# Another token layout for k and v from unit 6 on, and a load behind a store

## The chip, the core and the metric

The kernel runs on one core of a Trainium2 chip. The metric is the device time of one execution in microseconds; the time before is the median of 3 runs. A profile of one further execution goes with it. The engines are named as in the profile: PE is TensorE's matmul, PEld its weight load, DVE is VectorE, ACT is ScalarE, POOL is GpSimd, SP is SyncE, which here only issues DMAs.

## What is computed

The first half is a retention layer: for each of 4 batches and 8 heads, over 768 tokens of 64 features, a 64 x 64 state is decayed and updated, and a query reads it.

```python
gamma = 1.0 - 2.0 ** (-5.0 - np.arange(H))
for t in range(S):
    state = gamma[None, :, None, None] * state + np.einsum('bhd,bhe->bhde', k[:, :, t], v[:, :, t])
    y[:, :, t] = scale * np.einsum('bhd,bhde->bhe', q[:, :, t], state)
```

The second half takes y as 3072 tokens of 512 features through a feed-forward layer: `h = x @ w_in` (512 to 2048), `g = max(h, 0) + alpha * min(h, 0)`, and `g @ w_out` (2048 to 512). Inputs and output are float32.

## The kernel before

**Units and blocks.** A unit (`u`, 0 to 11) is 256 tokens of one batch, three units to a batch. Inside a unit there are two chunks of 128 tokens (`c`). A block (`n`, 0 to 5) is two units, 512 tokens, and is what the feed-forward layer takes at once. While PE works on the feed-forward of block n, the attention of the units of block n + 1 (`u0 = 2 * (n + 1)` and `u0 + 1`) is put in between: the feed-forward parts are generators, `tick(gen, m)` emits m matmuls of them. The order of the program is the order on each engine and each DMA queue; everything is written out by hand.

**A unit's preparation.** `load` brings q, k and v of a unit from DRAM by SP, one DMA of 512 KB each (the first units in halves). Partition p of the staged tile holds tokens 2p and 2p + 1 of the unit, all 8 heads; a run of 512 contiguous bytes per head. So partitions 0 to 63 hold the first chunk and 64 to 127 the second (`rows(c)`), and r = 0 or 1 tells a partition's two tokens apart. `rescale` multiplies q and k with powers of gamma from the table `tab` and casts them to float16 (`kdq`); `cast_v` casts v (`vx`). From unit 4 on this is POOL's work. `turn_dma` transposes `kdq` into `kq` with a DMA on SP (the earlier units with PE in `turn_pe`), so that features lie on partitions. `kdq`, `kq` and `vx` have 4 buffers each, the staged tiles 3.

**A unit's attention.** All of it uses 64 x 64 quarters of PE's array, four matmuls at a time (two chunks c, two heads a of a pair p):

- `sum_mm` (L215): the state's update of each chunk, k against v, 64 columns.
- `score_mm` (L268): for each half r of a chunk's keys, the 64 keys against all 128 queries of the chunk; 16 matmuls a call, two calls (`hh`) a unit.
- `masks` (L280): DVE multiplies the scores of 512 columns, both halves r, with the causal mask `mi`; four a unit.
- `out_mm`: the state's part (L298, whole array), then the masked scores against v (L313), 32 matmuls of 128 columns, added up in PSUM.
- `state_sum` (L237 to L241) adds and decays the running state on DVE and POOL; `state_copy` puts it into float16 tiles `tg`.

The queries' order inside a chunk is all even tokens, then all odd ones; `take_y` (ACT) puts the output back into place in `xT`.

**The feed-forward.** `ffn1` (L378) makes 16 tiles of h in 64 matmuls, ACT and DVE apply the activation (L389, L391). For block 0 `ffn2` does the second product; from block 1 on `ffn2_seven` (L464) does it as seven products of 16 matmuls in place of eight, with sums of g made by `g_sums` (L362). Their results are stored by SP (L489, `store`): output tile (0,0) in the second product, then (1,1), (1,0) and (0,1). The output tiles `os` have three buffers.

**SP's queue.** For block 1 it holds, in this order: the transposes of units 4 and 5, the loads of units 6 and 7, the four stores of block 1. From block 2 to 3: transpose of `u0`, load of `u0 + 2`, transpose of `u0 + 1`, load of `u0 + 3`, four stores. A DMA that waits holds up what is queued behind it.

Of the kernel before, what the change touches and what calls it, by code (L numbers as in the profile page):

```python
# [10 lines left out]
F16 = mybir.dt.float16  # L11
# [10 lines left out]
def kernel(  # L22
# [10 lines left out]
    nc = tc.nc  # L33
# [3 lines left out]
    NP = H // 2  # L37


    U = 256  # L40
    UPB = S // U
    NU = B * UPB
# [6 lines left out]


    OQ, OD, OI = 2 * H, 4 * H, 4 * H + NP
    NTAB = OI + NFT
    tab_np = np.zeros((128, NTAB), dtype=np.float64)
    for h in range(H):
        for r in range(2):
            j = 2 * (p_ar % 64) + r
            tab_np[:, 2 * h + r] = g64[h] ** (127.0 - j)
            tab_np[:, OQ + 2 * h + r] = scale * g64[h] ** (j + 1.0 - 128.0)
    for p in range(NP):
        tab_np[0:64, OD + p] = g64[2 * p] ** 128  # L60
# [10 lines left out]
    mi = sbp.tile([128, 512], F16, tag="mi", name="mi")  # L71
    mask = mi[:, 0:256].rearrange("p (r i) -> p r i", r=2)
    ident = mi[:, 256:384]
    dec = tab[:, OD : OD + NP].unsqueeze(2).to_broadcast([128, NP, 64])
    alpha_sb = sbp.tile([NFT, 128], FP, tag="alpha", name="alpha")
    spin = sbp.tile([128, 512], F16, tag="spin", name="spin")
# [33 lines left out]
    def hold(ins):  # L110
        if held:
            tc.add_manual_dep(
                ins.ins,
                held.pop().ins.name,
                mybir.DependencyInfo(
                    mybir.DependencyClass.Sync, mybir.DependencyReason.DATA
                ),
                reason="loads behind weights",
            )

    def load(u, parts="kqv"):
        b, c = divmod(u, UPB)
        t = staged.setdefault(u, {})
        for nm in parts:
            src = {"k": k, "q": q, "v": v}[nm[0]]
            if nm[0] not in t:
                t[nm[0]] = sbp.tile(
                    [128, H, 2 * D], FP, tag=f"{nm[0]}s", bufs=3, name=f"{nm[0]}s{u}"
                )
            h = slice(0, H) if len(nm) == 1 else slice(4 * int(nm[1]), 4 * int(nm[1]) + 4)  # L130
            hold(
                nc.sync.dma_start(  # L132
                    out=t[nm[0]][:, h, :],
                    in_=src[b, h, U * c : U * c + U, :].rearrange(
                        "h (p r) d -> p h (r d)", r=2
                    ),
                )
            )

    def unit(u):  # L140
        if u not in prepped:
            prepped[u] = (
                sbp.tile([128, 2, 2, H, D], F16, tag="kdq", bufs=4, name=f"kdq{u}"),
                sbp.tile([128, 4 * NP, 128], F16, tag="kq", bufs=4, name=f"kq{u}"),
                sbp.tile([128, H, 2, D], F16, tag="vx", bufs=4, name=f"vx{u}"),
            )
        return prepped[u]

    def rescale(eng, u, t, h0, h1):
        kdq = unit(u)[0]  # L150
        at = OQ * t
        return eng.tensor_tensor(  # L152
            out=kdq[:, t, :, h0:h1, :].rearrange("p r h d -> p h r d"),
            in0=staged[u]["kq"[t]][:, h0:h1, :].rearrange("p h (r d) -> p h r d", r=2),
            in1=tab[:, at + 2 * h0 : at + 2 * h1]
            .rearrange("p (h r) -> p h r", r=2)
            .unsqueeze(3)
            .to_broadcast([128, h1 - h0, 2, D]),
            op=MULT,
        )  # L160
# [13 lines left out]
    def turn_pe(u, hh, bank):  # L174
# [17 lines left out]
            bias=0.0,  # L192
            scale=1.0,
        )

    def rows(x):
        return slice(64 * x, 64 * x + 64)
# [29 lines left out]
    def state(u, c, eng, copy="gg"):  # L227

        state_copy(state_sum(u, c, eng), copy)
# [28 lines left out]
    def score_mm(u, hh, banks):  # L258
        _, kq, _ = prepped[u]
        kv = kq.rearrange("p (t r a) i -> p t r a i", t=2, r=2)  # L260
        scs = [ps(banks[0], "sca"), ps(banks[1], "scb")]
        for r in range(2):
            for pp in range(2):
                p = 2 * hh + pp
                for c in range(2):
                    for a in range(2):
                        at = 256 * r + 128 * pp
                        nc.tensor.matmul(  # L268
                            out=scs[a][rows(c), at : at + 128],
                            lhsT=kv[rows(a), 0, r, p, rows(c)],  # L270
                            rhs=qmove(kq, a, c, p),
                            start=True,
                            stop=True,
                        )
        live[u, hh] = scs

    def masks(u, hh, parts=(0, 1)):
        for a in parts:
            m2 = sbp.tile([128, 2, 2, 128], F16, tag=f"m2{a}{hh}", bufs=2, name=f"m2{a}{hh}")
            i = nc.vector.tensor_tensor(  # L280
                out=m2,
                in0=live[u, hh][a].rearrange("p (r a i) -> p r a i", r=2, a=2),
                in1=mask.unsqueeze(2).to_broadcast([128, 2, 2, 128]),
                op=MULT,
            )
            live[u, hh][a] = m2
        return i

    def out_mm(u, banks, evict=True):
        _, kq, vx = prepped[u]  # L290
        ys = [ps(banks[0], "y0"), ps(banks[1], "y1")]
        inter = [(u, c) in tgs for c in range(2)]
        assert inter == [u % UPB > 0, True]

        for c in range(2):
            for p in range(NP):
                if inter[c]:
                    nc.tensor.matmul(  # L298
                        out=ys[c][:, 128 * p : 128 * p + 128],
                        lhsT=tgs[u, c][:, p, :],  # L300
                        rhs=kq.rearrange("p (t r a) i -> p t r a i", t=2, r=2)[
                            :, 1, :, p, rows(c)
                        ],
                        start=(p == 0),
                        stop=False,
                        skip_group_check=True,
                    )
        for p in range(NP):
            m2s = live[u, p // 2]
            for r in range(2):  # L310
                for c in range(2):
                    for a in range(2):
                        nc.tensor.matmul(  # L313
                            out=ys[c][rows(a), 128 * p : 128 * p + 128],
                            lhsT=vx[rows(c), 2 * p + a, r, :],
                            rhs=m2s[a][rows(c), r, p % 2, :],
                            start=(r == 0 and p == 0 and not inter[c]),
                            stop=(r == 1),
                            skip_group_check=True,
                        )  # L320
        live[u] = ys
        if evict:
            take_y(u, (0, 1))
# [237 lines left out]
    load(1, ("k0", "q0", "k1", "q1", "v0", "v1"))  # L561
    V.memset(spin, 1.0)
    V.memset(mi, 1.0)
    V.memset(warm, 0.0)
    A.activation(out=warm, in_=warm, func=RELU, bias=0.0, scale=-1.0)

# [4 lines left out]
    for x in range(2):  # L571
        m = mi[rows(x), 0:256].rearrange("p (j i t) -> p j i t", j=2, i=2)
        G.affine_select(
            out=m, in_=m, pattern=[[-1, 2], [1, 2], [2, 64]], compare_op=NOT_LESS,
            fill=0.0, base=0, channel_multiplier=-2,
        )
    for t in tgbuf:
        V.memset(t, 0.0)

# [116 lines left out]
    turn_dma(4)  # L696
    turn_dma(5)
    load(6)
    load(7)
    tick(half)  # L700


    for n in range(1, NBLK):
# [17 lines left out]
        if more:  # L721
            tick(gen, 8)
            sum_mm(u0, (2, 3))
            sum_mm(u0 + 1, (2, 3), half=1)
            score_mm(u0, 0, (4, 5))
            score_mm(u0, 1, (6, 7))
            state(u0, 0, G)
            masks(u0, 0)
            s01 = state_sum(u0, 1, G)
            masks(u0, 1, (0,))  # L730
            s10 = state_sum(u0 + 1, 0, G)
            masks(u0, 1, (1,))
# [50 lines left out]
```

## Time and profile before

| what | value |
|---|---|
| median of 3 runs | 204.73 us (204.58 to 204.78) |
| the profiled execution | 206.04 us, span 204.3 us |
| PE busy | 195.2 us (96%), 2314 matmuls |
| DVE busy | 157.0 us (77%) |
| ACT, POOL busy | 101.9 us (50%), 83.3 us (41%) |
| granted TensorE clock | 1.000 |
| chain that ended last | PE 73%, DMA 16%, DVE 3%, POOL 2% |
| `score_mm` matmuls (L268) | 384 of 64 columns by 128, 4 at a time |
| masks (L280) | 48, about 683 ns each |
| unit loads of 512 KB | ks 4.6, qs 5.5, vs 6.4 us from issue to landing (median) |
| transposes by DMA | 8, 3.8 us to landing (median) |

The span runs from the first to the last instruction; the time of the execution has what lies around it as well. A digit in the slices is the busy share of a fortieth of the span in tenths. A line of the chain or of a timeline gives the start, the length, the engine, the line and, with "x", how many instructions were merged. A matmul's length is its whole passage; what a stream of them costs is read from the distance of their starts.

### The profile page before, as it was taken

What the parts mean: (1) busy time and instruction counts of PE and PEld (TensorE: products, weight loads), DVE (VectorE), ACT (ScalarE), POOL (GpSimd) and SP (SyncE); (2) the same over time, 40 slices, a digit from 0 to 9 for tenths busy, and PEclk for the clock granted to TensorE, in tenths of its full rate; (3) what the DMA queues carried; (4) which work ended last, traced back from release to release, by engine and by line L of the source; (5) the groups of instructions that cost most, each with busy time, mean ns of one, the idle gap of its engine ahead of it and who ended that gap; (6) DMA issues with size and microseconds to landing.
All of it is one profiled execution on the core that took longest, in us unless ns stands there. A gap on an engine that the chain in (4) does not pass through costs nothing.

```text
span 204.3 us, 5491 instructions
## 1 busy us (share of the span) xinstructions
PE 195.2 (96%) x2314; PEld 128.2 (63%) x2314; DVE 157.0 (77%) x246; ACT 101.9 (50%) x169; POOL 83.3 (41%) x96
## 2 busy tenths in 40 slices
PE   7789997999999999999999999999999999999993
PEld 2457543566574788744788644788544888545882
DVE  7794985646899999189998289996489995589841
ACT  2465665236376333477353466333476254466311
POOL 2289117480269553970065960165930250000000
PEclk9999999999999999999999999999999999999999
DMA  5998999599997799399911499910570011200004
GB/s 158 337 234 134 185 253 235 157 249 173 299 346 223 153 340 304 110 258 304 284 46 41 149 250 281 300 55 22 176 166 0 3 52 57 103 0 0 21 33 154
DMA packets 64696, 33.94 MB, mean 166 GB/s; under 512 B 18064, under 2 KB 64160, under 8 KB 64672
## 3 DMA queue, kind: packets, MB, share of 16 engines
q1 hardware_dynamic: 60272, 29.37, 50.0%
q0 software_dynamic: 4224, 4.19, 13.4%
q8 instruction: 18, 0.29, 0.6%
q10 hardware_dynamic: 176, 0.03, 0.1%
q14 instruction: 6, 0.05, 0.1%
HBM read 27.30 MB, written 6.29 MB: 164 GB/s over the span
## 4 chain that ended last, share of the span: by engine, by line
PE 73%; DMA 16%; DVE 3%; POOL 2%; SPq 2%; issue 2%; ACT 0%; POOLq 0%; DVEq 0%
PE hps L378 32%; PE ox L464 16%; PE oy L464 11%; DMA qs<-in_q_dram 6%; PE ops L416 5%; DMA wout<-in_moe_w_out_dram 4%; DMA win<-in_moe_w_in_dram 4%; DMA ks<-in_k_dram 3%; PE y L313 2%; SPq L132 2%; PE sca L268 2%; PE y L298 1%; POOL tf L241 1%; PE st L215 1%; PE oz L464 1%
## 5 line engine op out<-in xcount | busy, mean ns | idle before, releaser
L378 PE MATMUL hps<-xT,win 128*128 128x512 f16 (+1 forms) x432 | 84.5, 355 | 0.1
L391 DVE SCALAR_TENSOR_TENSOR gt<-hm,oma,hps 128x512 f16<-128x512 f32 (+1 forms) x108 | 70.8, 685 | 13.6 <-ACT hm L389 8.1
L389 ACT ACTIVATE hm<-hps 128x512 f32<-128x512 f32 x96 | 57.3, 597 | 33.6 <-PE hps L378 31.4
L378 PEld LDWEIGHTS <-win 128*128 128x128 f16 x432 | 42.0, 98 | 40.3 <-DMA win<-in_moe_w_in_dram 0.8
L464 PEld LDWEIGHTS <-gs 128*128 128x128 f16 x320 | 31.0, 98 | 3.9
L241 POOL TENSOR_TENSOR tf<-ss,tab 128x256 f32<-128x256 f32 x16 | 12.2, 765 | 35.7 <-DVE ss L240 34.7
L464 PEld LDWEIGHTS <-gt 128*128 128x128 f16 x240 | 22.8, 98 | 4.8
L152 POOL TENSOR_TENSOR kdq<-ks,tab 128x1024 f16<-128x1024 f32 (+1 forms) x10 | 17.3, 1729 | 18.8 <-issue 9.8
L480 ACT ACTIVATE cu<-ox 128x512 f32<-128x512 f32 (+1 forms) x18 | 9.5, 526 | 29.9 <-PE ox L464 29.7
L256 POOL CAST tg<-tf 64x256 f16<-64x256 f32 x29 | 14.2, 488 | 20.0 <-DVE tf L237 18.6
L485 DVE TENSOR_TENSOR os<-oy,cu 128x512 f32<-128x512 f32 x14 | 9.6, 689 | 16.2 <-PE oy L464 13.7
L152 POOL TENSOR_TENSOR kdq<-qs,tab 128x1024 f16<-128x1024 f32 (+1 forms) x13 | 20.7, 1594 | 1.9 <-DMA qs<-in_q_dram 1.9
L280 DVE TENSOR_TENSOR m<-sca,mi 128x512 f16<-128x512 f32 x24 | 16.4, 684 | 4.2 <-PE scb L268 4.2
L464 PE MATMUL ox<-wsum,gs 128*128 128x256 f16 x160 | 19.1, 273 | 0.0
L331 ACT ACTIVATE xT<-y 128x512 f16<-128x512 f32 x24 | 16.2, 741 | 5.6 <-PE y L313 5.5
L280 DVE TENSOR_TENSOR m<-scb,mi 128x512 f16<-128x512 f32 x24 | 16.3, 681 | 0.0
L416 PE MATMUL ops<-wout,gt 128*128 128x512 f16 x64 | 15.2, 380 | 0.2 <-DMA wout<-in_moe_w_out_dram 0.2
L168 POOL CAST vx<-vs 128x1024 f16<-128x1024 f32 (+1 forms) x13 | 12.5, 973 | 5.6 <-DMA vs<-in_v_dram 5.6
L362 DVE TENSOR_TENSOR gs<-gt 128x1024 f16<-128x1024 f16 (+1 forms) x14 | 12.9, 922 | 0.3
L254 ACT ACTIVATE tg<-tf 64x256 f16<-64x256 f32 x11 | 4.6, 414 | 15.6 <-POOL tf L241 10.4
L188 ACT ACTIVATE kq<-trb 128x1024 f16<-128x1024 f16 x8 | 8.2, 1024 | 6.7 <-PE trb L182 6.5
L464 PE MATMUL ox<-wout,gt 128*128 128x256 f16 x80 | 10.4, 274 | 0.0
(50 smaller groups left out, 175.1 us busy)
## 6 DMA issues: line engine op xcount, KB each, us to landing
out_dram<-os SPq DMA_DIRECT2D x21, 256.0 KB, 2.3
vs<-in_v_dram SPq DMA_DIRECT2D x10, 512.0 KB, 6.4
ks<-in_k_dram SPq DMA_DIRECT2D x8, 512.0 KB, 4.6
qs<-in_q_dram SPq DMA_DIRECT2D x8, 512.0 KB, 5.5
ks<-in_k_dram SPq DMA_DIRECT2D x8, 256.0 KB, 4.7
qs<-in_q_dram SPq DMA_DIRECT2D x8, 256.0 KB, 4.8
win<-in_moe_w_in_dram POOLq DMA_DIRECT2D x4, 512.0 KB, 8.0
wout<-in_moe_w_out_dram POOLq DMA_DIRECT2D x4, 512.0 KB, 8.5
```

Of the source, the lines that this page charges most:

```text
L152: return eng.tensor_tensor(out=kdq[:, t, :, h0:h1, :].rearrange("p r h d -> p h r d"), in0=staged[u]["kq"[t]][:, h0:h1, :].rearrange("p h ...
L168: eng.tensor_copy(out=o, in_=i)
L241: eng.tensor_tensor(out=t, in0=ss, in1=dec, op=MULT)
L256: nc.gpsimd.tensor_copy(out=o, in_=i)
L280: i = nc.vector.tensor_tensor(out=m2, in0=live[u, hh][a].rearrange("p (r a i) -> p r a i", r=2, a=2), in1=mask.unsqueeze(2).to_broadcast([ ...
L331: nc.scalar.activation(out=xT[n][:, ul, :, 128 * c : 128 * c + 128].rearrange("k a (p r) -> k a r p", r=2), in_=ys[c].rearrange("k (a r p) ...
L362: return nc.vector.tensor_tensor(out=o, in0=a, in1=b, op=op)
L378: nc.tensor.matmul(out=hps[:, f, :].rearrange("p (u t) -> p u t", t=U), lhsT=w_in_all[:, hp, 128 * (f0 + f) : 128 * (f0 + f) + 128], rhs=x ...
L389: nc.scalar.activation(out=hm, in_=hps, func=RELU, bias=0.0, scale=-1.0)
L391: nc.vector.scalar_tensor_tensor(out=gt[:, f0 + f, U * lo : U * hi], in0=hm[:, f, :], scalar=oma_sb[:, f0 + f : f0 + f + 1], in1=hps[:, f, :],
L416: nc.tensor.matmul(out=opss[tq], lhsT=gt[:, ft, 128 * tq : 128 * tq + 128], rhs=w_out_all[:, ft, :], start=(ft == 0), stop=(ft == NFT - 1),)
L464: nc.tensor.matmul(out=o[1][m], lhsT=lhs(f, m), rhs=rhs(f), start=(first and f == 0 and (m == 0 or o[0] is None)), stop=(f == HF - 1), ski ...
```

## The change

From `SPLIT = 6` on, that is for units 6 to 11:

- k and v are loaded in another layout. Partition p of the lower half holds tokens p and p + 64 of the first chunk, the upper half those of the second chunk. Each of the two tensors comes in 4 DMAs, one for each chunk (x) and half of its tokens (y), on 64 partitions, with 256 contiguous bytes a head and 128 KB a DMA. q keeps its layout and its one DMA.
- r = 1 now means the second 64 tokens of a chunk. No query of the first 64 sees them, so `score_mm` and `out_mm` take only the 64 later queries for r = 1. In the query order that is the columns 32 to 63 of the even and of the odd tokens: two pieces of 32 columns in what `score_mm` reads and in what `out_mm` adds to. The scores of r = 1 lie at column 256 with 64 columns a pair.
- `masks` multiplies 384 columns in place of 512, with a mask of its own, `mj`, that is made at the start by one memset on DVE and four selects on POOL.
- `rescale` of k takes other powers of gamma, a further 16 columns of the table.

For all units: `kdq`, `kq` and `vx` have 3 buffers in place of 4. And the load of unit 7 is no longer issued right behind that of unit 6, but in the loop's first pass (n = 1), where the emitted products have put the first store of block 1 on SP's queue ahead of it.

```diff
+    SPLIT = 6
...
-    NTAB = OI + NFT
+    O2 = OI + NFT
+    NTAB = O2 + 2 * H
...
+            tab_np[:, O2 + 2 * h + r] = g64[h] ** (127.0 - (p_ar % 64 + 64 * r))
...
+            if u >= SPLIT and nm != "q":
+                for x in range(2):
+                    for y in range(2):
+                        at = U * c + 128 * x + 64 * y
+                        nc.sync.dma_start(
+                            out=t[nm][rows(x), :, D * y : D * y + D],
+                            in_=src[b, :, at : at + 64, :].rearrange("h p d -> p h d"),
+                        )
+                continue
...
-                sbp.tile([128, 2, 2, H, D], F16, tag="kdq", bufs=4, name=f"kdq{u}"),
-                sbp.tile([128, 4 * NP, 128], F16, tag="kq", bufs=4, name=f"kq{u}"),
-                sbp.tile([128, H, 2, D], F16, tag="vx", bufs=4, name=f"vx{u}"),
+                sbp.tile([128, 2, 2, H, D], F16, tag="kdq", bufs=3, name=f"kdq{u}"),
+                sbp.tile([128, 4 * NP, 128], F16, tag="kq", bufs=3, name=f"kq{u}"),
+                sbp.tile([128, H, 2, D], F16, tag="vx", bufs=3, name=f"vx{u}"),
...
-        at = OQ * t
+        at = OQ if t else (O2 if u >= SPLIT else 0)
...
-                        at = 256 * r + 128 * pp
+                        at, n, q = 256 * r + 128 * pp, 128, qmove(kq, a, c, p)
+                        if u >= SPLIT and r == 1:
+                            at, n, q = 256 + 64 * pp, 64, q[:, :, 32:64]
                         nc.tensor.matmul(
-                            out=scs[a][rows(c), at : at + 128],
+                            out=scs[a][rows(c), at : at + n],
                             lhsT=kv[rows(a), 0, r, p, rows(c)],
-                            rhs=qmove(kq, a, c, p),
+                            rhs=q,
...
+            m2 = sbp.tile([128, 512], F16, tag=f"m2{a}{hh}", bufs=2, name=f"m2{a}{hh}")
+            if u >= SPLIT:
+                i = nc.vector.tensor_tensor(
+                    out=m2[:, 0:384], in0=live[u, hh][a][:, 0:384], in1=mj, op=MULT
+                )
...
+                        o = ys[c][rows(a), 128 * p : 128 * p + 128]
+                        at, n = 256 * r + 128 * (p % 2), 128
+                        if u >= SPLIT and r == 1:
+                            at, n = 256 + 64 * (p % 2), 64
+                            o = o.rearrange("p (r i) -> p r i", r=2)[:, :, 32:64]
                         nc.tensor.matmul(
-                            out=ys[c][rows(a), 128 * p : 128 * p + 128],
+                            out=o,
                             lhsT=vx[rows(c), 2 * p + a, r, :],
-                            rhs=m2s[a][rows(c), r, p % 2, :],
+                            rhs=m2s[a][rows(c), at : at + n],
...
     V.memset(mi, 1.0)
+    V.memset(mj, 1.0)
     V.memset(warm, 0.0)
...
+        for lo, n in ((0, 64), (256, 32)):
+            m = mj[rows(x), lo : lo + 4 * n].rearrange("p (a i t) -> p a i t", a=2, i=2)
+            G.affine_select(
+                out=m, in_=m, pattern=[[0, 2], [1, 2], [2, n]], compare_op=NOT_LESS,
+                fill=0.0, base=0, channel_multiplier=-1,
+            )
...
     load(6)
-    load(7)
     tick(half)
...
             tick(gen, 17)
+            if n == 1:
+                load(7)
             state(u0 + 1, 1, G)
```

More of the change, by code (lines that the diff above doesn't have):

```diff
@@ L73 @@
     ident = mi[:, 256:384]
+    mj = sbp.tile([128, 512], F16, tag="mj", name="mj")[:, 0:384]
     dec = tab[:, OD : OD + NP].unsqueeze(2).to_broadcast([128, NP, 64])
@@ L119, in hold, with rows @@
             )
+    def rows(x):
+        return slice(64 * x, 64 * x + 64)
     def load(u, parts="kqv"):
@@ L194, in turn_pe @@
         )
-    def rows(x):
-        return slice(64 * x, 64 * x + 64)
     def qmove(kq, a, c, p):
@@ L278, in masks @@
         for a in parts:
[L279 to L285, printed above, removed]
+            m2 = sbp.tile([128, 512], F16, tag=f"m2{a}{hh}", bufs=2, name=f"m2{a}{hh}")
[3 more added lines that the diff above has]
+                )
+            else:
+                i = nc.vector.tensor_tensor(
+                    out=m2.rearrange("p (r a i) -> p r a i", r=2, a=2),
+                    in0=live[u, hh][a].rearrange("p (r a i) -> p r a i", r=2, a=2),
+                    in1=mask.unsqueeze(2).to_broadcast([128, 2, 2, 128]),
+                    op=MULT,
+                )
             live[u, hh][a] = m2
@@ L576 @@
         )
+        for lo, n in ((0, 64), (256, 32)):
[3 more added lines that the diff above has]
+                fill=0.0, base=0, channel_multiplier=-1,
+            )
     for t in tgbuf:
```

## The prediction

> **What bounds the kernel now.** I read the page's slices first, then the chain that ended last, then the timelines of TensorE, VectorE and SP around one block.
>
> ```profile
> span 204.3 us, 5491 instructions
> ...
> PE   7789997999999999999999999999999999999993
> ...
> DVE  7794985646899999189998289996489995589841
> ...
> PEclk9999999999999999999999999999999999999999
> DMA  5998999599997799399911499910570011200004
> ```
>
> From about 60 us on, PE stands at 9 in every slice but the last, at full granted clock, while DMA falls to 0 or 1 in many slices. The chain, for the block that starts at 115 us:
>
> ```profile
> 115.12 13.81 PE hps L378 x64
> 128.93 0.91 PE ox L464 x8
> 129.84 0.62 PE st L215 x42
> ...
> 135.83 0.57 PE y L313 x32
> ...
> 144.84 1.30 PE hps L378 x6
> ```
>
> No other engine stands between two PE pieces there: 29.7 us of matmul after matmul. So in units 6 to 11 PE time taken out comes off the end, and work of other engines counts only if it becomes late. Now the small matmuls (start, length, count):
>
> ```profile
> 99.81 0.71 PE L215 MATMUL st<-vx,kdq 64*64 64x64 f16 x64
> ...
> 106.06 0.22 PE L268 MATMUL sca<-kq 64*64 64x128 f16 x2
> ...
> 106.12 0.22 PE L268 MATMUL sca<-kq 64*64 64x128 f16 x2
> ...
> 106.29 0.22 PE L268 MATMUL sca<-kq 64*64 64x128 f16 x1
> 106.49 0.21 PE L268 MATMUL scb<-kq 64*64 64x128 f16 x1
> ```
>
> Four 64x64 matmuls on the four quarters of the array start together, and the next four 0.056 us later (106.06, 106.12, ...) when 128 columns move. With 64 columns (`sum_mm`, L215), 64 matmuls have 0.71 - 0.19 (length of one) = 0.52 us between first and last start, which is 15.75 steps: 0.033 us per four. The 0.20 us between 106.29 and 106.49 is a stall; VectorE shows whose:
>
> ```profile
> 102.09 0.68 DVE L280 TENSOR_TENSOR m<-sca,mi 128x512 f16<-128x512 f32 x1
> 102.69 0.68 DVE L280 TENSOR_TENSOR m<-scb,mi 128x512 f16<-128x512 f32 x1
> 103.28 0.41 DVE L240 TENSOR_TENSOR ss<-tf,st 128x256 f32<-128x256 f32 x1
> ...
> 106.03 0.41 DVE L240 TENSOR_TENSOR ss<-tf,st 128x256 f32<-128x256 f32 x1
> ```
>
> The second half of unit 7's scores (L268) needs banks 2 and 3, which the last `ss` reads until 106.44. Last, SP's queue in that block:
>
> ```profile
> 86.39 1.74 SPq L172 DMA_TRANSPOSE kq<-kdq  x1
> 88.18 0.57 SPq L132 DMA_DIRECT2D ks<-in_k_dram  x1
> ...
> 89.53 1.59 SPq L132 DMA_DIRECT2D vs<-in_v_dram  x1
> 91.23 4.49 SPq L172 DMA_TRANSPOSE kq<-kdq  x1
> 95.77 0.57 SPq L132 DMA_DIRECT2D ks<-in_k_dram  x1
> ```
>
> **The change part by part.**
>
> *Matmuls (removed columns).* In units 6 to 11 the r = 1 half of `score_mm` and `out_mm` moves 64 columns in place of 128: 16 of 32 matmuls each, that is 4 groups of four in each of the two, 8 groups a unit, 48 groups. 56 - 33 = 23 ns each: 48 x 0.023 = 1.10 us, all on the path. The trace has no matmul whose moving operand or PSUM output is two pieces of 32 columns. Bounds: nothing gained, at the price of today's 128-column row; or half of today's row, 28 ns each, 1.34 us. I take 1.10, since L215 has the same 64x64 tiles, 64 columns and a weight load for each matmul. A loss is excluded for the matmuls: fewer columns at the same count.
>
> *Masks.* 24 masks go from 512 to 384 columns. Back to back, 512-column ones start 0.60 us apart (102.09, 102.69, 103.28), and what follows a 256-column `ss` starts 0.33 later; so 128 columns are worth 0.135 us and 24 masks 3.2 us of VectorE. In most blocks that only widens slack. In the block of units 6 and 7, four masks stand before the last `ss`. One step of this chain goes through POOL's `tf`, so not all of 0.54 arrives: walking it, `ss` ends near 106.03. PE, itself 10 groups x 0.023 = 0.23 us earlier, gets there near 106.1. The stall of 0.20 us goes; next late would be PE itself. Bounds 0 to 0.20; I take 0.20.
>
> *Loads of 6 to 11.* Of each unit k and v become 4 DMAs each of 64 partitions in 256 B pieces: 9 issues where there were 3. An unhindered issue takes SP 0.37 to 0.57 us (L132), so six more cost 2.2 to 3.4 us of SP. The trace's packet records give 27 ns for a 512 B packet, 18 for the 256 B packets of the transposes, 46 for 1 KB ones. A tensor is 64 packets per DMA engine today, 1.73 us, and 128 after: 2.3 us at 18 ns, 3.5 if a 256 B packet costs what a 512 B one does. So a load of three tensors goes from 5.2 to 6.3 (at worst 8.6) us: +1.1 to +3.4. On the path: nothing, by these covers. Unit 7's transpose is issued behind unit 8's load at 91.23, its packets end at 97.25, and PE first needs the result at 106.06: 8.8 us of cover. Unit 9's end at 127.11 against 136.23: 9.1. Unit 9's load issue ends at 98.57 and the next store is only ready at 106.14, 7.6 us of SP time; a later store hurts only when an output buffer (three) comes round. If the cover is gone, each of the two blocks with loads pays the excess once on PE.
>
> *Eight in flight.* Each SP DMA waits for the semaphore of the eighth DMA before it on SP (8 take turns in the records). Unit 8's seventh issue then waits for the transpose of unit 6, which lands about 3.7 us after its issue, by 90.1, before that seventh issue could start (88.2 + 6 x 0.5 = 91.2). Nothing.
>
> *Unit 7's load behind the first store of block 1.* That store is issued at 76.70, now queued behind the load; the load moves from 71.65 to some 77.1. Queued behind it on SP: three stores (81.92 to 85.91) and unit 6's transpose (86.39). Nine issues at 0.57 end at 82.2; by data (6.3 us) near 83.5; the first of those stores may go 1.5 us late, the last none. POOL takes k of unit 7 at 86.12, q at 87.99, v at 89.83, all landed by 85 or so. If data came 5 us later still, POOL would pass it to `sum_mm` of unit 7, which stands at 100.1, over 9 us behind POOL's 90.86. Nothing.
>
> *Three buffers for `kdq`, `kq`, `vx`.* Unit 5's rescale (63.56) now needs unit 2 finished (41.7), unit 7's (86.12) unit 4 (76.5), unit 9's (116.0) unit 6 (106.2), unit 11's (145.3) unit 8 (136.4). Nothing.
>
> *Start.* One more memset (0.54 us with its gap) ahead of `warm` and the zeroed `tg`: VectorE's first rescale goes from 4.01 to some 4.2. POOL gets four more selects, at most 2 x 0.42 + 2 x 0.29 = 1.4 us, in an idle stretch to 8.81. POOL at work can slow a rescale (L152 on VectorE: 0.98 at 9.41 beside a POOL cast, 0.69 alone), 0.3 more. VectorE waits 0.94 us for k before 6.37 and 0.33 before 9.41, which takes the lag of up to 0.5. Bounds 0 to 0.5 (chain: win DMA, unit 2's load); I take 0.
>
> Sum: -1.10 - 0.20 = -1.3 us. The profiled execution has a span of 204.3 and 206.04 us in all, 1.31 above the median 204.73; its span would be 203.0, the median 203.4.
>
> The Trainium skill speaks against the loads: "DMA: Bandwidth & Descriptors" (Specifications) wants 512 B or more for line rate, and "SBUF — State Buffer" (Can I just issue two DMAs to hit both halves?) says that transfers to the two partition halves serialize, and 64 partitions reach half the ports, 196 GB/s. This trace has no load on 64 partitions; its 256 B transposes (18 ns) cover all 128. By 196 GB/s I estimate 2.7 us a tensor, which leaves the sum as it is.
>
> **The rivals.**
>
> *A: the split loads starve the transposes: slower.* Place: unit 7's `kq` at 106.06, again unit 9's at 136.23. It decides once unit 8's load lasts 8.8 us longer, that is, two tensors of 128 packets an engine at (8.8 / 2 + 1.73) / 128 = 48 ns, what a 1 KB packet takes now. Against it: 18 ns for 256 B. For it: no such load is in the trace; if a DMA on half the partitions used half the engines without overlap and at 27 ns a packet, a tensor takes 6.9 us, the load 15.5, 10.3 more; the excess over the cover is 1.5 us in one block and 1.2 in the next: 204.73 - 1.3 + 2.7 = 206.1. The two pages' rule would have to be this severe.
>
> *B: no change.* The half matmuls still cost 56 ns a group (two pieces of 32 columns, weights loaded as often), and only the stall goes: 204.5. Against it: L215's 33 ns.
>
> *C: part.* Only `score_mm` or only `out_mm` shrinks, or the start's 0.5 is paid: -0.6 to -0.9, 203.8 to 204.2.
>
> **How the numbers follow.** Forecast 0.58, C 0.17, B 0.10, A and anything like it 0.15. Below 0.2% (0.41 us) this kernel can't be told from no change. Faster, below 204.32: forecast and C, 0.74. Same: B, with the little excess A can have, 0.11. Slower: 0.15. The range starts at 1.34 + 0.20 with some 0.3 for looser waits, 202.9, and reaches over C and B to 204.7; beyond it lie A and a little below, 2 in 10.
>
> **What would show it.** Right: score and out matmuls with 64 columns at about 33 ns per four; masks near 0.55 us; no 0.2 us stall in the middle of unit 7's scores; the block from 115 us shorter by 0.37 us; PE at 9 in all later slices. Wrong: PE waiting at L268 or L215 for `kq`, `kdq` or `vx`, POOL waiting for k or v DMAs, or a first half of the kernel that is longer.

## The result, and the profile after

The changed kernel takes 203.57 us (median of 22 runs, 202.6 to 205.49) beside 205.0 us for the kernel before in the same comparison (22 runs): ratio 0.9915, 95% interval 0.9894 to 0.9937. On two later occasions the same pair gave 0.9961 (0.9935 to 0.9988) and 0.9940 (0.9916 to 0.9964). The three intervals share only a narrow strip around 0.9936, that is 1.3 us less; why they scatter is taken up below. The prediction was 203.4 us, 1.3 less than before.

The profiled execution took 203.86 us, with a span of 202.2. Page of the changed kernel, head and slices:

```profile
span 202.2 us, 5547 instructions
...
PE   6688999999999999999999999999999999999993
...
DVE  7695887645899999189998289995489984589851
...
PEclk9999999999999999999999999999999999999999
DMA  5999999699997698998995499990570011200014
```

PE still stands at 9 to the last slice but one, at full clock. What bounds the kernel has not changed. DMA is fuller than before in the middle, where the split loads run. The chain of the changed kernel, for the block of units 8 and 9:

```profile
113.86 13.81 PE hps L404 x64
127.67 0.91 PE ox L490 x8
128.58 0.62 PE st L229 x44
...
134.54 0.47 PE y L339 x32
...
143.30 13.81 PE hps L404 x64
```

From the start of one ffn1 to the next it is 143.30 - 113.86 = 29.44 us; in the trace of before the first matmuls of the same two stand at 114.96 and 144.68, 29.72 apart. A call of `out_mm` takes 0.47 us in the chain for its 32 small matmuls where it took 0.57.

The table splits the span at the first `sum_mm` matmul of units 4, 6, 8 and 10 (each stands at the head of a block's attention), at the first matmul of the last ffn1, and at the end. Each row is one profiled execution, worked out from the starts of these matmuls in its trace.

| trace | to unit 4 | block 1 | block 2 | block 3 | to last ffn1 | to the end |
|---|---|---|---|---|---|---|
| before | 69.19 | 30.61 | 29.96 | 29.73 | 15.13 | 29.70 |
| before, second trace | 67.55 | 30.61 | 29.97 | 29.73 | 15.13 | 29.74 |
| before, third trace | 67.43 | 30.61 | 29.97 | 29.73 | 15.13 | 29.74 |
| changed | 68.43 | 30.62 | 29.46 | 29.44 | 14.74 | 29.47 |
| changed, second trace | 68.44 | 30.61 | 29.41 | 29.40 | 14.74 | 29.48 |
| changed, third trace | 67.74 | 30.61 | 29.46 | 29.39 | 14.74 | 29.48 |

Read it by columns. Blocks 2 and 3 and the stretch to the last ffn1 hold the changed units 6 to 11, and each kernel repeats them within 0.06 us. Their sum is 74.83 us before and 73.59 (mean of three) after: the change is worth 1.24 us there. The first column swings by 1.76 us in the kernel before alone. The first two profiles are 2.18 us apart in span, and 0.76 of that lies in this column, where the trace of before happened to be a bad one.

Where the 1.24 us come from is seen in unit 7's scores, at the place whose stall the prediction showed. PE's timeline of the changed kernel (start, length, count; of `scb` only the line at the place of the stall):

```profile
105.22 0.22 PE L284 MATMUL sca<-kq 64*64 64x128 f16 x2
...
105.28 0.22 PE L284 MATMUL sca<-kq 64*64 64x128 f16 x2
...
105.33 0.19 PE L284 MATMUL sca<-kq 64*64 64x64 f16 x2
...
105.36 0.20 PE L284 MATMUL sca<-kq 64*64 64x64 f16 x2
...
105.39 0.22 PE L284 MATMUL sca<-kq 64*64 64x128 f16 x2
105.40 0.22 PE L284 MATMUL scb<-kq 64*64 64x128 f16 x2
```

Groups of 128 columns are 0.05 to 0.06 us from the next group, groups of 64 columns 0.03. Before, PE stood for 0.20 us inside the fifth group, between its first `sca` matmul (106.29) and `scb` (106.49). Here the two stand at 105.39 and 105.40, without a gap. VectorE's timeline of the changed kernel tells why:

```profile
101.33 0.55 DVE L297 TENSOR_TENSOR m<-sca,mj 128x384 f16<-128x384 f32 x1
101.79 0.55 DVE L297 TENSOR_TENSOR m<-scb,mj 128x384 f16<-128x384 f32 x1
102.25 0.41 DVE L254 TENSOR_TENSOR ss<-tf,st 128x256 f32<-128x256 f32 x1
...
104.26 0.68 DVE L511 TENSOR_TENSOR os<-oy,cu 128x512 f32<-128x512 f32 x1
104.86 0.41 DVE L254 TENSOR_TENSOR ss<-tf,st 128x256 f32<-128x256 f32 x1
```

Masks of 384 columns start 0.46 us apart, and the last `ss` is through at 104.86 + 0.41 = 105.27, ahead of the fifth group. (The line of `os` is read with SP's queue below.)

What the loads cost stands in SP's queue of the changed kernel:

```profile
86.48 2.36 SPq L189 DMA_TRANSPOSE kq<-kdq  x1
88.89 2.66 SPq L143 DMA_DIRECT2D ks<-in_k_dram  x4
91.60 0.62 SPq L149 DMA_DIRECT2D qs<-in_q_dram  x1
92.28 3.84 SPq L143 DMA_DIRECT2D vs<-in_v_dram  x4
96.23 2.44 SPq L189 DMA_TRANSPOSE kq<-kdq  x1
98.71 3.11 SPq L143 DMA_DIRECT2D ks<-in_k_dram  x4
...
106.12 1.10 SPq L515 DMA_DIRECT2D out_dram<-os  x1
```

Unit 8's load keeps SP from 88.89 to 96.23 where it had taken from 88.18 to 91.23, and unit 7's transpose stands 5.00 us later (96.23 for 91.23). It lands at 100.73 (97.77 before) and is first used at 105.22: the cover has gone from 8.3 us to 4.5. In the second and third trace of the changed kernel it is 1.5 and 2.3 us (landing at 103.68 for 105.14, at 102.25 for 104.52). Unit 9's load ends its issues at 106.02, and the next store follows at 106.12. Its output tile was ready at 104.26 + 0.68 = 104.94, so this store goes 1.2 us late. Nobody waits for it here, but SP has no free time left between these loads and the store.

### The profile page after: what moved, and what is told of

Its sections match the earlier page's. It is cut to its first block, busy times and chain, and to the rows that moved or that the text cites. A ratio compares the mean times of both kernels' runs of the same rounds, so it can differ in the third digit from the quotient of the medians.

```text
span 202.2 us, 5547 instructions
## 1 busy us (share of the span) xinstructions
PE 194.0 (96%) x2314; PEld 127.8 (63%) x2314; DVE 154.5 (76%) x247; ACT 101.8 (50%) x169; POOL 85.2 (42%) x100
## 3 DMA queue, kind: packets, MB, share of 16 engines
q1 hardware_dynamic: 73136, 29.37, 54.8%
## 4 chain that ended last, share of the span: by engine, by line
PE 81%; DMA 7%; DVE 3%; POOL 3%; issue 2%; SPq 2%; ACT 1%; DVEq 0%; POOLq 0%
PE hps L404 39%; PE ox L490 16%; PE oy L490 11%; PE ops L442 5%; DMA wout<-in_moe_w_out_dram 4%; DMA ks<-in_k_dram 3%; PE y L339 2%; PE y L319 2%; SPq L149 2%; PE sca L284 2%; POOL tf L255 1%; PE st L229 1%; PE oz L490 1%; DVE ss L254 1%; DVE m L301 1%
## 5 line engine op out<-in xcount | busy, mean ns | idle before, releaser
L301 DVE TENSOR_TENSOR m<-sca,mi 128x512 f16<-128x512 f32 x12 | 8.2, 685 | 3.0 <-PE scb L284 3.0
L96 PE MATMUL kps<-spin 128*128 128x512 f16 x25 | 8.3, 471 | 1.8 <-DVE spin L588 1.5
```

What stands on the lines that cost most here:

```text
L301: i = nc.vector.tensor_tensor(out=m2.rearrange("p (r a i) -> p r a i", r=2, a=2), in0=live[u, hh][a].rearrange("p (r a i) -> p r a i", r=2 ...
```

## Experiments

Every kernel but the repeats is the changed one with the edit shown ("..." marks what is left out of it); none leaves work out. "Ratio" is to the kernel before, with a 95% interval. Distances are those of the table above.

**1. Without the new layout** (`split12`). Start, three buffers and the later load of unit 7 stay; no unit is "from `SPLIT` on".

```diff
-    SPLIT = 6
+    SPLIT = 12
```

> SPLIT = 12: no unit takes the new layout, so what is left of the change is the start (one memset, four selects, a wider table), three buffers for kdq, kq and vx, and unit 7's load behind the first store of block 1. My theory (the gain is PE's 1.1 us of columns and 0.2 us of a stall in block 2): nothing left, ratio 0.998 to 1.002 to the kernel before, the stretch from the first matmul of block 1's ffn1 to the end as long as before (146.3 us in its profile). Rival (a part of the gain, about 0.75 us, comes from a later start that lets unit 2's load pass the w_out DMA, as the two profiles' first 57 us suggest): ratio near 0.996, and the matmuls of block 1's ffn1 begin again near 57.2 us in place of 58.0.

Measured: ratio 1.0002 (0.9983 to 1.0022). Blocks 1, 2, 3 and the stretch to the last ffn1 are 30.61, 29.96, 29.74 and 15.13 us, those of the kernel before to 0.01. The rest of the edit (three buffers, load behind the store, new mask and table) is worth nothing in these stretches. The first column is 67.83: the bad first third of the first trace of before is gone without any of the change's gain.

**2. New layout and loads, old sizes** (`fullcols`). k and v come in 4 DMAs each, but r = 1 meets all 128 queries, and the masks have 512 columns.

```diff
-                        if u >= SPLIT and r == 1:
-                            at, n, q = 256 + 64 * pp, 64, q[:, :, 32:64]
...
-                    out=m2[:, 0:384], in0=live[u, hh][a][:, 0:384], in1=mj, op=MULT
+                    out=m2, in0=live[u, hh][a], in1=mj, op=MULT
...
-                        if u >= SPLIT and r == 1:
-                            at, n = 256 + 64 * (p % 2), 64
-                            o = o.rearrange("p (r i) -> p r i", r=2)[:, :, 32:64]
...
```

> New layout from unit 6 with all its DMAs, but the r = 1 half moves all 128 columns in score_mm and out_mm and the masks cover 512 columns (zeros where a query sees no key). My theory: the loads are hidden, so the time is that of the kernel before, ratio 0.998 to 1.002, and the 0.2 us stall in unit 7's scores is back. Rival (the 36 more DMAs cost time on PE or SP that the halved columns pay back): slower than before by that cost, ratio over 1.002, with PE waiting at the scores of unit 7 or 9 or for an output buffer.

Measured: ratio 0.9978 (0.9957 to 0.9998), median 204.5; blocks 1 to 3 and the next stretch 30.61, 29.96, 29.74, 15.13. So the split loads cost nothing on the path, and the whole gain hangs on the columns. The stall in unit 7's scores is back, 0.10 us of it (from 105.98 to 106.08). The ratio just under 1 is not in these stretches: the trace has its small difference in the last one (29.46 for 29.70).

**3. Only `out_mm` shrinks** (`out_only`). `score_mm` keeps 128 columns, the masks 512.

```diff
-                        if u >= SPLIT and r == 1:
-                            at, n, q = 256 + 64 * pp, 64, q[:, :, 32:64]
...
-                            at, n = 256 + 64 * (p % 2), 64
...
-                            rhs=m2s[a][rows(c), at : at + n],
+                            rhs=m2s[a][rows(c), at : at + n]
+                            if u < SPLIT or r == 0
+                            else m2s[a][rows(c), at : at + n].rearrange(
+                                "p (r i) -> p r i", r=2
+                            )[:, :, 32:64],
...
```

> Only out_mm takes 64 columns for r = 1; score_mm moves all 128 and the masks cover 512 columns again. My theory: half of the matmul gain, 24 groups at 23 ns = 0.55 us, 0.18 to 0.19 us in each of the three blocks, and the 0.2 us stall in unit 7's scores stays, since the masks are long again: block 2's stretch 29.77, block 3's 29.53 us. If the shorter masks do not matter, the stall goes here too and block 2's stretch is 29.6.

Measured: ratio 0.9968 (0.9946 to 0.9991). Block 3 is 29.59 and the next stretch 14.94: 0.14 and 0.19 us saved, half of what the full change saves. Block 2 is only 0.10 shorter. PE's timeline of this kernel in unit 7's scores:

```profile
105.35 0.22 PE L282 MATMUL sca<-kq 64*64 64x128 f16 x2
...
105.41 0.22 PE L282 MATMUL sca<-kq 64*64 64x128 f16 x1
105.63 0.21 PE L282 MATMUL scb<-kq 64*64 64x128 f16 x1
```

The stall is there, 0.22 us between 105.41 and 105.63. PE came earlier, `ss` behind four long masks did not, so the stall took back part of what the matmuls had saved. This shows that the shorter masks are needed in block 2. In the two later stretches half of the gain is there without them, which leaves them no share of it.

**4. Unit 7's load right behind unit 6's** (`load7_back`).

```diff
     load(6)
+    load(7)
     tick(half)
...
-            if n == 1:
-                load(7)
```

> As the changed kernel, but unit 7's load is issued right behind unit 6's again. The 18 issues at 0.68 us take SP from 68.3 to about 80.6, so block 1's first store goes 4.7 us later. My theory: an output buffer comes round only with the fourth store, no one waits: same time as the changed kernel within 0.2%, ratio to before 0.990 to 0.994. Rival (the move is what keeps the stores, and with them VectorE's output sums and PE, on time): 0.5 us or more slower than the changed kernel, with VectorE waiting for a store's DMA before its sum in block 1.

Measured: ratio 0.997 (0.9946 to 0.9994); block 1 is 31.16 us, 0.55 longer than in all other rows of the table. I had expected that nobody waits. SP's queue and VectorE of this kernel:

```profile
82.50 4.85 SPq L515 DMA_DIRECT2D out_dram<-os  x4
```

```profile
80.08 0.69 DVE L511 TENSOR_TENSOR os<-oy,cu 128x512 f32<-128x512 f32 x1
86.26 0.69 DVE L511 TENSOR_TENSOR os<-oy,cu 128x512 f32<-128x512 f32 x1 [5.49 <-DMA out_dram<-os]
```

With eighteen load DMAs in a row on SP the first store of block 1 goes out at 82.50 (75.89 in the changed kernel). The block's fourth output sum needs one of three `os` buffers back and waits 5.49 us for that store to land. PE idles 0.39 us, up to 87.00, until that sum is done, and VectorE begins ffn1's activations behind it at 86.87 in place of 85.93. In all, the stretch is 0.55 us longer. So the move of the load is no decoration: with the split loads it is what keeps block 1 at 30.61. How much it would be worth with three whole DMAs a load was not tried; before, with both loads in front, block 1 was 30.61 as well.

**5. The new layout from unit 4 on** (`split4`), and for unit 4 besides 6 to 11 (`unit4`).

```diff
-    SPLIT = 6
+    SPLIT = 4
```

> SPLIT = 4: units 4 and 5 take the new layout too. My theory: 16 more groups at 23 ns, 0.37 us, and in block 1 VectorE's four shorter masks (0.54 us) shorten the stall of 0.65 us before out_mm of unit 4; together 0.7 to 0.9 us faster than the changed kernel, ratio to before 0.986 to 0.990. Rival (there the DMAs have no cover: loads 4 and 5 run from 48 to 57 us while DMA is busy, and 12 more issues at 0.68 us make SP 8 us longer before the stores of block 0 and the transposes of units 4 and 5): the transposes or POOL's rescale come late, PE waits before the scores of unit 4 at 69 us, no faster or slower than the changed kernel.

```diff
+    NEW = (4, 6, 7, 8, 9, 10, 11)
...
-                        if u >= SPLIT and r == 1:
+                        if u in NEW and r == 1:
```

(and so in the other four places where `u >= SPLIT` stands)

> The new layout for units 4 and 6 to 11, unit 5 as before. My theory: unit 4's four masks are what PE waits for in block 1 (0.65 us), and only their 0.54 us and 8 groups at 24 ns count there; six more issues in place of twelve keep unit 4's transpose in time (it landed at 66.7 of 68.4 needed in the changed kernel, 69.7 with units 4 and 5). So 0.6 to 0.8 us faster than the changed kernel, from unit 4's sum_mm to unit 6's 29.9 to 30.0 us in place of 30.6. Rival: load 4's longer DMAs push the transpose back as in the run with SPLIT = 4, PE waits up to 1 us before unit 4's scores, same as or slower than the changed kernel.

Measured: `split4` 0.9968 (0.9943 to 0.9993), block 1 30.97; `unit4` 0.9946 (0.9919 to 0.9974), block 1 30.39, short of what I had expected of it. PE's weight loads and SP in `split4`:

```profile
69.78 0.43 PEld L284 LDWEIGHTS <-kq 64*64 64x64 f16 x32 [1.34 <-DMA kq<-kdq]
```

```profile
62.55 6.86 SPq L189 DMA_TRANSPOSE kq<-kdq  x2
69.51 2.65 SPq L143 DMA_DIRECT2D ks<-in_k_dram  x4
```

The transposes of units 4 and 5 hold SP for 6.86 us. Unit 4's lands at 69.74, where in the changed kernel it lands at 66.69, and PEld waits 1.34 us for `kq`. So what rival A feared, a transpose that comes late, happens here, at a unit whose transpose had 2.2 us of cover. But it doesn't come late on SP's queue: it is issued at 62.55 (62.86 in the changed kernel) and takes 7.2 us to land in place of 3.8. What slows the transpose itself is open. In `unit4` it lands at 69.60, so the six issues saved did not keep it in time; the weight loads' gap ahead of these scores is some 0.3 us, and 0.22 us of block 1 is gained; the time can't be told from that of the changed kernel.

**6. The same packets in twice as many DMAs** (`eight_dmas`). Each k or v tensor comes in 8 DMAs of 64 KB, with the same 256 B pieces on the same 64 partitions.

```diff
-                        nc.sync.dma_start(
-                            out=t[nm][rows(x), :, D * y : D * y + D],
-                            in_=src[b, :, at : at + 64, :].rearrange("h p d -> p h d"),
-                        )
+                        for g in range(2):
+                            nc.sync.dma_start(
+                                out=t[nm][rows(x), 4 * g : 4 * g + 4, D * y : D * y + D],
+                                in_=src[b, 4 * g : 4 * g + 4, at : at + 64, :].rearrange(
+                                    "h p d -> p h d"
+                                ),
+                            )
```

> Units 6 to 11: each of k and v in 8 DMAs of 64 KB in place of 4 of 128 KB, with the same 256 B packets and the same bytes; only the number of issues doubles, 17 a load. If SP's issue (0.68 us each) is what makes the loads long: a load takes 11.6 us of SP in place of 7.2, unit 7's transpose lands near 105 to 107 where PE needs it at 105.2, the first store of block 2 goes 10 us late, VectorE waits for it before the fourth output sum and PE stalls at the start of block 3's ffn1: 4 us or more slower than the changed kernel. If the packets are what makes them long: about the changed kernel's time, and loads of 10 us from first issue to last landing, as now.

Measured: 218.85 us, ratio 1.0687 (1.0659 to 1.0716). Block 2 is 41.45 us, 12.0 longer than in the changed kernel; blocks 1 and 3 are 0.8 and 2.1 longer, the latter with a wait of PE of 1.95 us for a late output sum. PE and SP of this kernel:

```profile
115.70 0.31 PE L287 MATMUL sca<-kq 64*64 64x128 f16 x1 [9.78 <-DMA kq<-kdq]
```

```profile
94.67 3.48 SPq L192 DMA_TRANSPOSE kq<-kdq  x1
98.20 6.18 SPq L144 DMA_DIRECT2D ks<-in_k_dram  x8
104.42 2.09 SPq L152 DMA_DIRECT2D qs<-in_q_dram  x1
106.56 5.21 SPq L144 DMA_DIRECT2D vs<-in_v_dram  x8
111.88 1.67 SPq L192 DMA_TRANSPOSE kq<-kdq  x1
```

A load takes SP 13.7 us (98.20 to 111.88), and unit 7's transpose stands behind it. The queue was late before that: unit 6's transpose stands at 94.67 (86.48 in the changed kernel), since the loads of units 6 and 7 have twice as many issues too. The delays of the three loads add up. PE waits 9.78 us at exactly the place that rival A named. Yet the packets take no longer. SP's DMA queue, first in the changed kernel and then in this one (packets, MB, share of 16 engines' span):

```profile
q1 hardware_dynamic: 73136, 29.37, 54.8%
```

```profile
q1 hardware_dynamic: 73904, 29.37, 50.7%
```

54.8% of 202.2 us is 110.8, 50.7% of 217.2 is 110.1. Same bytes, same packet time, and the end comes 15 us later: from 9 issues a load to 17 it is the number of issues on SP that makes it longer. At 9 issues this run doesn't part the two. There SP takes 7.3 us a load, and its packets, by an estimate from 256 pieces of 256 B per DMA engine at 18.9 ns and 64 of 512 B at 27, take 6.6.

**7. What the start costs** (`start_late`, with `after_third`, the changed kernel, beside it). The new mask, its selects and the 16 new columns of the table are moved from the start to just ahead of unit 6's load.

```diff
-    V.memset(mj, 1.0)
...
     turn_dma(4)
     turn_dma(5)
+    nc.sync.dma_start(out=tab2, in_=tab_h.ap()[:, O2 : O2 + 2 * H])
+    V.memset(mj, 1.0)
+    for x in range(2):
+        for lo, n in ((0, 64), (256, 32)):
...
     load(6)
```

> The new mask, its four selects on POOL and the sixteen new columns of the table (a small DMA of their own) are moved from the start to just ahead of unit 6's load; the rest is the changed kernel. The prediction put their cost at the start at nothing: then the feed-forward of block 0 begins between 18.4 and 19.2 us as in the other traces, and the time is that of the changed kernel within 0.2 us (203.4 to 203.8). Rival: they cost 0.3 to 0.4 us there (block 0's first ffn1 matmul stood at 18.39, 18.56 and 18.43 us in three traces of the kernel before, at 18.80 in the mean of eight traces of kernels that make the mask at the start): then it begins at 18.4 to 18.6 us and the time is 0.3 to 0.4 us below that of the changed kernel in the same call. From unit 4's sum_mm to the end both give 133.6 to 134.0 us.

> The changed kernel once more, as the other side of the run with the late mask and for a second interval. By the stretches measured so far, the change is worth 1.2 us from unit 5 on, up to 1.5 with the end of the kernel: a ratio of 0.993 to 0.994, unless something before unit 4 takes a part back (0.3 to 0.4 us: 0.995).

Measured: 203.06 us, ratio 0.9921 (0.9892 to 0.995), beside 203.38 us and 0.9940 (0.9916 to 0.9964). The first matmul of block 0's ffn1 starts at 18.48 us, and at 18.69 in the changed kernel beside it. VectorE at the start, with the late mask and then in the changed kernel:

```profile
3.93 0.69 DVE L171 TENSOR_TENSOR kdq<-ks,tab 128x512 f16<-128x512 f32 x1 [0.27 <-DMA ks<-in_k_dram]
...
6.49 0.69 DVE L171 TENSOR_TENSOR kdq<-ks,tab 128x512 f16<-128x512 f32 x1 [1.13 <-DMA ks<-in_k_dram]
```

```profile
3.98 0.80 DVE L169 TENSOR_TENSOR kdq<-ks,tab 128x512 f16<-128x512 f32 x1
...
6.67 0.69 DVE L169 TENSOR_TENSOR kdq<-ks,tab 128x512 f16<-128x512 f32 x1 [1.19 <-DMA ks<-in_k_dram]
```

The rescale beside POOL's selects is 0.11 us longer, and then VectorE waits over a microsecond for the next k in both: its own delay is covered, as the prediction had it. What is later is the landing of k (6.67 for 6.49), and whether the start causes that is open: it lay at 6.18, 6.37 and 6.57 in the three traces of before. The difference in time, 0.32 us, is what the rival expected, but the intervals overlap nearly whole. So a cost of the start between 0 and 0.3 us is left open, and this version, whose block 1 is 0.13 us longer in its trace (30.74), isn't shown to be faster than the changed kernel. All traces together lean to a cost. With the mask made at the start, ffn1's first matmul stands at 18.39 to 19.16 us (mean of ten traces 18.78); without, at 18.39 to 18.55 (mean of four 18.46). And the table's first column is 67.74 or more in those ten, 67.43, 67.48 and 67.55 in three of these four.

**8. The same kernels again** (`before_again`, `before_third`, `after_again`), to see which columns of the table scatter by themselves.

> The kernel before, profiled again. If the 0.76 us by which the first two profiles differ ahead of unit 4's sum_mm is scatter of the DMA-bound first third, this profile has its sum_mm of unit 4 elsewhere than 69.19, somewhere between 67.8 and 69.2 as in the runs so far, and the same stretches after it as the first one (30.61, 29.96, 29.73). If it is something that the change does, it is again near 69.2.

> The same once more, as a second look at the scatter: same expectation as for the first.

> The changed kernel itself, timed and profiled once more beside the next three. All theories: from the first sum_mm of unit 4 on the same stretches as in its first profile, 30.62, 29.46 and 29.44 us from one block's sum_mm to the next; ratio to before 0.990 to 0.995. What differs from the first profile should lie before unit 4's sum_mm, where the profiles so far differ by up to 1.4 us for the same program.

Measured: 204.43, 204.32 and 203.8 us, and the rows of the table. The first third of the two new traces of before is 1.64 and 1.76 us shorter than in the first one, where PE waited 1.08 us up to 33.98 for unit 2's rescale on POOL, and that for unit 2's q. Beside these two (spans 202.7 and 202.6 us) the first trace of the changed kernel (202.2) is only 0.5 us shorter, its third (201.4) 1.2; in the blocks behind, all of them say 1.2 or more. It is the first third that makes the time scatter, and with it the ratios.

Not tried: four buffers for `kdq`, `kq` and `vx` beside the new mask. That three buffers cost nothing rests on `split12`.

## Why the prediction was right, step by step

**Matmuls, -1.10 us: right.** The step said 48 groups at 23 ns. The 32 matmuls of an `out_mm` call take 0.47 us for 0.57, that is 0.10 for 4 groups, and `score_mm`'s groups stand 0.03 apart in place of 0.056: 24 to 25 ns a group, 1.15 to 1.2 us in all. Two pieces of 32 columns, the form that the trace of before didn't have, cost no more than 64 in a row. `fullcols` shows that the gain hangs on these columns, `out_only` that each of the two products has half of it. By blocks the prediction had 0.57, 0.37 and 0.37 us (stall included); measured, as means of three traces, are 0.52, 0.32 and 0.39, together 1.24 for 1.30. The two stretches without a stall give 0.72 us for 32 groups, 22 ns a group. So rival B (no gain from the columns) is refuted. Rival C's case of one product alone is what `out_only` made: 0.10 + 0.14 + 0.19 = 0.43 us in these stretches, a median of 204.31.

**Masks and the stall, -0.20 us: right.** The distance of two masks was predicted at 0.60 - 0.135 = 0.465 and is 0.46; `ss` was to end near 106.03 in the old time, and PE finds it done. `out_only` shows the counterpart: short `out_mm` with long masks and the stall stays, 0.22 us.

**Loads, nothing on the path: right in the sum, wrong in its size.** The step's term "an unhindered issue takes SP 0.37 to 0.57 us, so six more cost 2.2 to 3.4 us" was mis-sized. The small loads stand 0.68 us apart (88.89, 89.57, 90.25, 90.92) though each moves a quarter of the bytes, and with the waits among them a load takes SP 7.3 us in place of 3.05: 4.3 more. The same step's data part gave +1.1 us, at most +3.4: the last packet of unit 8's load lands 10.06 us after its first issue (98.95 - 88.89) for 7.63, 2.4 more, inside these bounds, and its last issue ends only at 96.12. The 7.6 us of SP time that the step had counted before the next store were more than used up: that store goes 1.2 us late, and no one waits for it. `eight_dmas` shows how near rival A lay: not by way of slow packets, which the prediction had named as what decides, but by way of SP's issues, which it had held for the cheap part. The step's 8.8 us of cover was in truth a budget of issues. Of it 1.5 to 4.5 us are left in the three traces, and eight more issues a load overdrew that by 9.78 us. So "nothing" was right with less margin than the step gave.

The Trainium skill, "DMA: Bandwidth & Descriptors" (Issuing engines are not separate DMA queues), calls the sequencer's time to initiate a DMA usually small relative to the DMA itself. Here it is not: 0.68 us of SP for 128 KB, whose packets take 512 / 16 x 18.9 ns = 0.6 us on each of the 16 DMA engines. As to the page that the prediction weighed, "SBUF — State Buffer" (Door 1: The DMA port swizzle) of the Trainium skill with 196 GB/s for 64 partitions, that is an estimate of 0.67 us for 128 KB. The trace is in line with it. The four v loads of unit 8 land at 97.58, 98.02, 98.47 and 98.95, only 0.46 us apart, but their packets overlap, so this distance is no rate. From 96.00 to 97.58, when nearly all packets were 256 B pieces and by their number these loads', the DMA engines moved 202 GB/s. Whether the half of the partitions sets this rate isn't shown: 256 B every 18.9 ns on 16 engines is 217 GB/s by itself.

**Eight in flight, three buffers: nothing, right.** By `split12` and `fullcols`, whose stretches are those of before.

**Unit 7's load behind the store: nothing, right, but for a reason that I had not seen.** Block 1 is 30.61 us before and after. I read this as a move without effect. `load7_back` shows that it isn't: with nine DMAs a load, the old place would cost 0.55 us by way of a store, an output buffer and VectorE. The move pays for the split of the loads.

**Start, 0 of 0 to 0.5: open** within 0 to 0.3, with the traces leaning to 0.3 (experiment 7).

**What the steps don't hold.** The last stretch is 0.2 to 0.3 us shorter in the three traces of the changed kernel. None of the change's work lies there, and PE's matmuls are the same. The last store takes 1.68 us from issue to landing in both (201.32 to 203.00 before, 199.37 to 201.05 after). The difference lies behind it: from this landing to the end it is 1.34 us before and 1.11 after. There SP goes through the eight semaphores of its DMAs one after the other, 0.06 us each. Eight of these waits follow the landing before, four after, because another semaphore has its turn for the last store: SP issues 79 DMAs before and 115 after. The other traces fit this. `split12` with 79 DMAs and `split4` with 127, both 7 above a multiple of eight, have the long form, and `fullcols` with 115 the short one, with no gain in its blocks. So these 0.24 us come from the number of DMAs and not from the columns.

With them the change is worth 1.5 us by the traces behind the first third; the three ratios say 0.8 to 1.7, and the first third, which scatters by more than the whole effect, stands between the two. The mechanism of the prediction is borne out by the stretches (1.24 for 1.30). That the median also fell by the forecast 1.3 us or so is in part luck: the 0.24 us at the end, which the sum doesn't have, and a cost of up to 0.3 at the start, which it put at nothing, about cancel.

## What to carry to other kernels

When PE is the bound and streams without gaps, price a cut in its work by the distance of starts in a row of the same tile form, not by an instruction's length: 56 and 33 ns a group gave the answer to 0.1 us, where a single matmul shows 0.22 and 0.19. Price a split load by the issues on the queue that carries it as well as by its packets, and count what else is in that queue: here the transposes were nearest to costing time, and the stores next, by way of their buffers. And before trusting a difference of two profiles, take a second profile of the old kernel and compare stretch by stretch: the stretches that repeat to 0.05 us told the change from the scatter at once.

## What was not expected of the hardware

- A DMA of 128 KB in 512 pieces of 256 B takes SP 0.63 us to issue, and the next starts 0.05 later; the 512 KB loads with 1,024 pieces of 512 B took 0.57 to 0.68 where nothing held them up, and eight DMAs of 64 KB with 256 pieces still 5.32 and 6.22 us, 0.66 to 0.78 each with their waits. So the cost is per DMA more than per byte.
- 256 B packets, those of loads and transposes together, take 18.9 ns on the average of the changed kernel's trace (18 were assumed). DMAs on 64 partitions landed 0.46 us apart while the DMA engines moved 202 GB/s: the distance of landings overstates the rate.
- A long wait costs more than its length. In `eight_dmas` the wait of 9.78 us made block 2 longer by 12.0. The windows of that kernel (busy time and count of PE, PEld, DVE, ACT and POOL, then the granted clock, the DMA share and GB/s):

```profile
105.90:108.00 2.10, 0.02 (x4) 0.00 (x0) 0.83 (x1) 1.33 (x2) 1.99 (x3) 1.00 0.23 35
108.00:110.00 2.00, 0.00 (x0) 0.00 (x0) 0.00 (x0) 0.00 (x0) 0.10 (x1) 0.83 1.05 294
110.00:112.00 2.00, 0.00 (x0) 0.00 (x0) 0.00 (x0) 0.00 (x0) 0.00 (x0) 0.50 0.62 138
...
118.00:120.00 2.00, 2.00 (x13) 1.52 (x12) 1.36 (x2) 0.00 (x0) 0.51 (x1) 0.61 0.43 98
120.00:122.00 2.00, 2.00 (x23) 1.74 (x21) 0.00 (x0) 0.34 (x1) 2.00 (x2) 1.00 0.70 193
```

The granted clock falls to 0.50 some 3.4 us after PE has stopped at 105.9 (the mean of 0.83 over 108 to 110 puts the step at 109.3). It is back at 119.6 (a mean of 0.61 over 118 to 120), 3.9 us after PE went on at 115.7: at half clock that is 1.9 us lost. From unit 7's first score to the next ffn1 it is 10.28 us, where the changed kernel takes 8.47. The Trainium skill, "TensorE: Matmul & The Clock Gate" (What's actually happening), has windows of about 3.4 us for both, and the trace agrees. In the prediction rival A was priced without it, since its wait was thought to be 1.5 us.
